# The first product by half tokens, earlier weight loads, and halo copies moved from GpSimd to VectorE

## The chip, the cores and the metric

The kernel runs on one core of a Trainium2 chip. The metric is the device time of one execution in microseconds (us). Here a profile's span is about 1.7 us shorter than the time of the same execution. Engines are named as in the profile: PE is TensorE's matmul unit, PEld its weight load, DVE is VectorE, ACT is ScalarE, POOL is GpSimd, SP is SyncE.

With each execution the mean granted TensorE clock over the span is given, 1.00 being full speed.

## The reference, cut to what matters

```python
xn = layernorm(x)                       # x: 2048 tokens x 1024, bf16
s  = attention(xn) @ wo                 # 32 heads, each token sees 8 tokens, 2 apart
g  = silu((silu(xn @ w1) * (xn @ w3)) @ w2)     # inner width 3584
return x + s * g
```

The attention of a token looks back at most 14 tokens. The kernel works on chunks of 512 tokens, so each chunk of keys and values carries a *halo*: the last few columns of the chunk before it, copied to the front of the tile.

## The kernel before

The large products are done as two-by-two block products with seven block products in place of eight, which needs sums of the inputs (`xs`, for example, are sums of blocks of the normalised x). The parts concerned:

```python
def spin(ps, n):                        # n dummy matmuls of 512 columns on zeros
    ...
def first_two(key, A, b11, b21, snap, e11, mid=lambda: None, busy=0):
    pa = []
    for g in range(2):
        pa.append(bank2(f"a{key}{g}"))
        spin(pa[g], busy if g == 0 else 0)
        for i in I:
            mm(pa[g][:, i], A[g][0][i], b11, True)
        act_copy(snap[g], pa[g][:])
    mid()
    ...
def halo(t, js):
    nc.gpsimd.tensor_copy(out=t[:, js, 0:HALO], in_=t[:, js, CH:CH + HALO])

def fetch_v(c, js):                     # called at the end of each half of values(c - 1)
    halo(vT, js)
    anchor["pool"] = nc.gpsimd.dma_start(out=vT[:, js, HALO:], in_=v_dram[c, :, js])
...
x_load(0)
wq0 = qkv_load(0, 0, slot(2, (4, D)))
x_load(1)
wq1 = qkv_load(0, 1, slot(6, (4, D)))
for st in range(NST):                   # normalise the four 128-token tiles
    (ln_act if st == 2 else ln_dve)(0, [st])
...
tps = [ln_tp(0, st, [], busy=(5, 0, 1, 1)[st]) for st in range(NST)]    # transposes on PE
for a in I:                             # copy the transposes out of PSUM
    ...
wk0 = qkv_load(1, 0, slot(8, (4, D)))
wk1 = qkv_load(1, 1, rows(0, 4).rearrange("p (k n) -> p k n", k=4))
...
TPE = ()
qkv_load(2, 0, wve[0][:])
for st in range(NST):                   # second chunk of x: normalise, transpose by DMA
    ln_dve(1, [st])
    ...
    if st == 1:
        qkv_load(2, 1, wve[1][:])
```

Near the end of the kernel, the step that PE waits for. One tile, `dsp`, gets a copy on ScalarE, an add on VectorE and a Silu on ScalarE; then the next such copy follows on ScalarE:

```python
def c22(gp):
    sp5 = k4(f"dsp{b}_{gp}")
    act_copy(sp5[:], pe[gp][:])
    with hp():
        anchor["v"] = nc.vector.tensor_add(sp5[:], pb[gp][:], sp5[:])
        silu(g_tile(b, 1, 1, gp), sp5[:])
```

## Time and profile before

| kernel before | value |
|---|---|
| median of the three runs | 726.93 us (725.63 to 726.95) |
| median of all 29 runs made beside the experiments | 726.25 us (725.3 to 727.53) |
| span of its profile | 725.4 us |
| PE busy | 715.2 us, 99% of the span |
| first useful matmul | 12.23 us |
| body (first product with `xs`) starts | 34.05 us |
| PE's part in the chain that ended last is over | 713.91 us (PE itself ends at 719.51) |

Three stretches have to be told apart: the *head*, up to 34 us, where input arrives, is normalised and transposed, and the first halves of three products run; the *body*, from the first matmul on `xs` to the end of PE's part in the chain that ended last, which lasted 679.86 us; and a tail of last sums and stores. Head, body and tail follow each other, so a gain in either of the first two is a gain in the time, unless the other takes it back.

### The profile page before, as it was taken

How to read it: one execution, taken by the hardware profiler on the slowest of the kernel's cores; microseconds unless marked ns; L12 is line 12 of the kernel's file. 1: busy time of each engine (PE TensorE's matmuls, PEld its weight loads, DVE VectorE, ACT ScalarE, POOL GpSimd, SP SyncE). 2: the span in 40 equal slices, each digit the busy share in tenths (PEclk: the TensorE clock that was granted, in tenths of full speed). 3: DMA queues.
4: the chain of work that ended last, by engine and by line, in shares of the span. 5: the costliest groups of instructions: out<-in, count | busy, mean ns of one | idle time of the engine just before them, and what ended most of it. 6: DMA issues, size and time to landing. Idle time of an engine off the chain costs nothing.

```text
span 725.4 us, 8725 instructions
## 1 busy us (share of the span) xinstructions
PE 715.2 (99%) x3335; PEld 344.1 (47%) x3335; DVE 622.8 (86%) x678; ACT 313.9 (43%) x325; POOL 111.7 (15%) x171
## 2 busy tenths in 40 slices
PE   8999999999999999999999999999999999999996
PEld 4655656554444444444444444444444444444442
DVE  8795879779879878978999999969859989978984
ACT  5654434356555556554545312034364573020233
POOL 0011100011310300332212010000434006020011
PEclk9999999999999999999999999999999999999999
DMA  9966156877755453566756556469799445564515
GB/s 325 278 155 171 59 188 215 266 237 255 225 176 180 145 174 116 178 189 199 248 166 229 184 160 219 144 203 379 175 282 321 144 136 160 167 195 140 188 27 111
DMA packets 120137, 139.77 MB, mean 193 GB/s; under 512 B 18592, under 2 KB 95392, under 8 KB 119456
## 3 DMA queue, kind: packets, MB, share of 16 engines
q1 hardware_dynamic: 105552, 97.27, 44.1%
q0 software_dynamic: 14544, 41.95, 18.8%
q8 instruction: 26, 0.43, 0.2%
q14 instruction: 15, 0.12, 0.1%
HBM read 96.21 MB, written 38.80 MB: 186 GB/s over the span
## 4 chain that ended last, share of the span: by engine, by line
PE 92%; DVE 3%; ACT 2%; DMA 1%; issue 1%; SPq 0%; DVEq 0%; ACTq 0%
PE bm L149 20%; PE am L149 13%; PE em L149 13%; PE db L149 10%; PE bq L149 9%; PE de L149 7%; PE da L149 7%; PE eq L149 5%; PE aq L149 3%; PE wb L149 2%; PE we L149 2%; PE wa L149 2%; DVE stats L250 1%; DMA wve<-in_A_wqkv_dram 1%; PE af L149 1%
## 5 line engine op out<-in xcount | busy, mean ns | idle before, releaser
L149 PEld LDWEIGHTS <-wring 128*128 128x128 f16 (+1 forms) x1824 | 187.9, 103 | 207.5 <-issue 1.9
L149 PEld LDWEIGHTS <-h_sb 128*128 128x128 f16 (+1 forms) x1056 | 109.6, 104 | 119.4 <-issue 2.0
L149 PE MATMUL bm<-xs,wring 128*128 128x512 f16 x504 | 117.4, 379 | 0.1
L149 PE MATMUL am<-xT,wring 128*128 128x512 bf16 x336 | 79.7, 379 | 0.1
L149 PE MATMUL db<-wring,h_sb 128*128 128x512 f16 x336 | 73.2, 379 | 0.0
L474 DVE TENSOR_TENSOR BC<-Ep,vT 128x2048 bf16<-128x2048 bf16 x56 | 66.7, 1219 | 0.1
L419 DVE TENSOR_TENSOR pt<-qt,kT 128x4096 bf16<-128x4096 bf16 x24 | 55.0, 2290 | 0.7
L657 DVE TENSOR_TENSOR um<-em,um 128x1024 f32<-128x1024 f32 x28 | 34.2, 1223 | 20.9 <-PE em L149 20.0
L659 ACT ACTIVATE g<-um 128x1024 bf16<-128x1024 f32 x28 | 29.6, 1057 | 48.2 <-DVE um L657 48.2
L149 PE MATMUL da<-wring,h_sb 128*128 128x512 bf16 x224 | 49.0, 379 | 0.0
L460 POOL DMA_DIRECT2D Ep<-pb x64 | 37.9, 599 | 53.7 <-DVE pb L456 46.6
L149 PE MATMUL bm<-h_sb,wring 128*128 128x512 f16 x168 | 39.7, 379 | 0.0
L149 PE MATMUL em<-xs,wring 128*128 128x512 f16 x168 | 39.7, 379 | 0.0
L149 PE MATMUL em<-xT,wring 128*128 128x512 bf16 x168 | 39.7, 379 | 0.0
L484 DVE TENSOR_TENSOR oT<-oT,BC 128x2048 bf16<-128x2048 bf16 x32 | 39.0, 1220 | 0.4
L159 ACT COPY bm<-am 128x1024 f32<-128x1024 f32 x28 | 27.9, 998 | 26.0 <-PE am L149 26.0
L159 ACT COPY pm<-em 128x1024 f32<-128x1024 f32 x28 | 28.4, 1013 | 20.1 <-PE em L149 20.1
L159 ACT COPY um<-bm 128x1024 f32<-128x1024 f32 x28 | 28.4, 1013 | 19.2 <-PE bm L149 19.2
L678 ACT CAST g<-bm 128x1024 bf16<-128x1024 f32 x28 | 28.3, 1010 | 17.4 <-PE bm L149 17.4
L672 DVE TENSOR_TENSOR h_sb<-bm,pm 128x1024 bf16<-128x1024 f32 x21 | 25.6, 1218 | 5.1 <-PE bm L149 5.0
L421 DVE TENSOR_TENSOR pt<-pt 128x2048 bf16<-128x2048 bf16 x24 | 29.3, 1222 | 0.4
L962 POOL DMA_DIRECT2D out_dram<-h_sb x12 | 15.1, 1512 | 94.7 <-DVE h_sb L961 94.6
(197 smaller groups left out, 1019.5 us busy)
## 6 DMA issues: line engine op xcount, KB each, us to landing
wring<-in_B_w_dram SPq DMA_DIRECT2D x61, 512.0 KB, 4.5
wring<-t_dram SPq DMA_DIRECT2D x16, 512.0 KB, 3.7
t_dram<-wring POOLq DMA_DIRECT2D x14, 512.0 KB, 4.6
wring<-t_dram SPq DMA_DIRECT2D x16, 384.0 KB, 5.1
wring<-in_B_w_dram SPq DMA_DIRECT2D x12, 384.0 KB, 4.0
wring<-in_A_x_dram SPq DMA_DIRECT2D x16, 256.0 KB, 4.7
Ep<-pb POOLq DMA_DIRECT2D x64, 64.0 KB, 4.6
wring<-in_A_wo_dram SPq DMA_DIRECT2D x8, 512.0 KB, 5.7
```

The source lines that it names most:

```text
L149: anchor["pe"] = nc.tensor.matmul(ps, lhsT=lhs[k], rhs=rhs[k], start=(first and k == 0), stop=(k == n - 1), skip_group_check=not first,)
L159: nc.scalar.copy(out=out_, in_=in_)
L419: nc.vector.tensor_mul(p_t[:], q[:], kT[:, :, o:o + CH])
L421: nc.vector.tensor_add(p_t[:, 0:4, :], p_t[:, 0:4, :], p_t[:, 4:8, :])
L460: nc.gpsimd.dma_start(out=pr[c][r:P:NR, :, sq * P:(sq + 1) * P], in_=pb[sq * 32:(sq + 1) * 32, :, :])
L474: nc.vector.tensor_mul(dst, E[:, w, :].unsqueeze(1).to_broadcast([P, n, CH]), vT[:, js, o:o + CH])
L484: nc.vector.tensor_add(A, A, B if w0 else C)
L657: v = nc.vector.tensor_add(su2[:], pe[:], su2[:])
L659: nc.scalar.activation(out=hl["g"][:, :, CH:], in_=su2[:], func=ACTF.Silu)
L672: anchor["v"] = nc.vector.tensor_add(h[:, :, CH:], pb[:], sp5[:])
L678: nc.scalar.copy(out=hl["g"][:, :, 0:CH], in_=pb[:])
L962: nc.gpsimd.dma_start(out=rows_, in_=g, accum_op=ALU.add)
```

## The change

The intent is to start the first product on two of the four token tiles while the other two are still being prepared, to have the weights there in time, and to take the halo copies off GpSimd.

```diff
     x_load(0)
     wq0 = qkv_load(0, 0, slot(2, (4, D)))
+    wq1 = qkv_load(0, 1, slot(6, (4, D)))
+    wk0 = qkv_load(1, 0, slot(8, (4, D)))
     x_load(1)
-    wq1 = qkv_load(0, 1, slot(6, (4, D)))
-    for st in range(NST):
-        (ln_act if st == 2 else ln_dve)(0, [st])
...
-    tps = [ln_tp(0, st, [], busy=(5, 0, 1, 1)[st]) for st in range(NST)]
...
+    ln_dve(0, [0])
+    ln_act(0, [1])
+    ln_dve(0, [2])
+    ln_dve(0, [3])
+    def p1(g, th):                      # a quarter of the first product: 256 tokens
...
+    spin_in(0, 0, 5)
+    tpose(0, 0); tpose(0, 1); untp(0, 0, dve_copy); untp(0, 1, sc_copy)
+    tpose(1, 0); tpose(1, 1); untp(1, 0, sc_copy);  untp(1, 1, sc_copy)
+    tpose(2, 0); tpose(2, 1); untp(2, 0, dve_copy)
+    p1(0, 0)
+    tpose(3, 0); tpose(3, 1); untp(3, 0, dve_copy); untp(2, 1, sc_copy); untp(3, 1, dve_copy)
+    p1(1, 0)
+    p1(0, 1)
+    p1(1, 1)
...
-    TPE = ()
-    qkv_load(2, 0, wve[0][:])
+    TPE = (3,)                          # one tile of the second chunk transposed by PE
+    for h in I:
+        qkv_load(2, h, wve[h][:])
...
     def halo(t, js):
-        nc.gpsimd.tensor_copy(out=t[:, js, 0:HALO], in_=t[:, js, CH:CH + HALO])
+        nc.vector.tensor_copy(out=t[:, js, 0:HALO], in_=t[:, js, CH:CH + HALO])
```

(The `tpose` and `untp` lines stand one to a line in the kernel.) Cut here: the root and reciprocal of the normalisation get high priority for the first two chunks, and the weight sums of `wq` are tied behind a copy of the transposes. Six dummy matmuls fall away, one each before the transposes of tiles 2 and 3 and four before the first product.

More of the change, by code (lines that the diff above doesn't have):

```diff
@@ L165, in flush, with first_two @@
             pend.pop(0)()
-    def first_two(key, A, b11, b21, snap, e11, mid=lambda: None, busy=0):
-        pa = []
+    def first_two(key, A, b11, b21, snap, e11, mid=lambda: None, pa=None):
+        have, pa = pa, pa or []
         for g in range(2):
-            pa.append(bank2(f"a{key}{g}"))
-            spin(pa[g], busy if g == 0 else 0)
-            for i in I:
-                mm(pa[g][:, i], A[g][0][i], b11, True)
-            act_copy(snap[g], pa[g][:])
+            if have is None:
+                pa.append(bank2(f"a{key}{g}"))
+                for i in I:
+                    mm(pa[g][:, i], A[g][0][i], b11, True)
+                act_copy(snap[g], pa[g][:])
         mid()
@@ L251, in ln_dve @@
             nc.vector.bn_aggr(out=mv[:, i, :], in_=stats[:])
-        nc.scalar.activation(out=rstd[:], in_=mv[:, :, 1], func=ACTF.Sqrt, bias=eps_t[:], scale=1.0)
-        nc.vector.reciprocal(out=rstd[:], in_=rstd[:])
+        with hp() if c < 2 else nullcontext():
+            nc.scalar.activation(out=rstd[:], in_=mv[:, :, 1], func=ACTF.Sqrt, bias=eps_t[:], scale=1.0)
+            nc.vector.reciprocal(out=rstd[:], in_=rstd[:])
         for i, st in enumerate(sts):
@@ L297, in xn_sums @@
         nc.vector.tensor_sub(o[:, 2], b22, b12)
-        nc.vector.tensor_sub(o[:, 3], b21, o[:, 1])
+        anchor["xs"] = nc.vector.tensor_sub(o[:, 3], b21, o[:, 1])
     def B_of(b11, b21, b22, o):
@@ L986 @@
     qt[0] = att_tile((NJ, CH), BF16, "qt0")
-    tps = [ln_tp(0, st, [], busy=(5, 0, 1, 1)[st]) for st in range(NST)]
-    for a in I:
-        for st in range(NST):
-            (nc.vector.tensor_copy if st < 2 else nc.scalar.copy)(
-                out=xT[:, a, :, st * P:(st + 1) * P], in_=tps[st][:, a].rearrange("p (k t) -> p k t", k=KH),
-            )
-    wk0 = qkv_load(1, 0, slot(8, (4, D)))
+    snap = [oT[:, i // 2, 4 * (i % 2):4 * (i % 2) + 4].rearrange("p j n -> p (j n)").bitcast(FP32).rearrange("p (i n) -> p i n", i=2) for i in range(4)]
@@ new lines, with tpose, untp @@
+    tpb = {}
+    def tpose(st, a):
+        key = a, st // 2
+        if key not in tpb:
+            tpb[key] = bank2(f"tp{a}{st // 2}")
+        tp = tpb[key]
+        for k in range(KH):
+            nc.tensor.matmul(
+                tp[:, st % 2, k * P:(k + 1) * P], lhsT=xt[0][:, st, (a * KH + k) * P:(a * KH + k + 1) * P], rhs=ident[:],
+                start=(k == 0), stop=(k == KH - 1), skip_group_check=True,
+            )
+    def untp(st, a, eng):
+        with hp():
+            r = eng(out=xT[:, a, :, st * P:(st + 1) * P], in_=tpb[a, st // 2][:, st % 2].rearrange("p (k t) -> p k t", k=KH))
+        if eng == dve_copy:
+            anchor["x"] = r
@@ new lines @@
+    dve_copy, sc_copy = nc.vector.tensor_copy, nc.scalar.copy
+    ln_dve(0, [0])
+    ln_act(0, [1])
+    ln_dve(0, [2])
+    ln_dve(0, [3])
+    pf = {}
+    def p1(g, th):
+        if g not in pf:
+            pf[g] = bank2(f"af0{g}")
+        cols = slice(th * 2 * P, (th + 1) * 2 * P)
+        w = wq0.rearrange("p k (c two j) -> p k two j c", two=2, j=4)
+        for i in I:
+            for k in range(KH):
+                nc.tensor.matmul(
+                    pf[g][:, i, cols], lhsT=w[:, k, 0, 2 * g + i, :], rhs=xT[:, 0, k, cols],
+                    start=(k == 0 and th == 0), stop=(k == KH - 1), skip_group_check=True,
+                )
+        act_copy(snap[g][:, :, cols], pf[g][:, :, cols])
@@ new lines, in spin_in @@
+    def spin_in(st, a, n):
+        tpb[a, st // 2] = bank2(f"tp{a}{st // 2}")
+        spin(tpb[a, st // 2], n)
+    spin_in(0, 0, 5)
+    tpose(0, 0)
+    tpose(0, 1)
+    untp(0, 0, dve_copy)
+    untp(0, 1, sc_copy)
+    tpose(1, 0)
+    tpose(1, 1)
+    untp(1, 0, sc_copy)
+    untp(1, 1, sc_copy)
+    tpose(2, 0)
+    tpose(2, 1)
+    untp(2, 0, dve_copy)
+    p1(0, 0)
+    tpose(3, 0)
+    tpose(3, 1)
+    untp(3, 0, dve_copy)
+    untp(2, 1, sc_copy)
+    untp(3, 1, dve_copy)
+    p1(1, 0)
@@ L1006 @@
                 )
-        if st == 1:
-            qkv_load(2, 1, wve[1][:])
     x_load(2)
@@ L1012 @@
     sq = [sq[:, q] for q in range(3)]
-    snap = [oT[:, i // 2, 4 * (i % 2):4 * (i % 2) + 4].rearrange("p j n -> p (j n)").bitcast(FP32).rearrange("p (i n) -> p i n", i=2) for i in range(4)]
     Bq = B0, B_of(xT1[0], xT1[1], xT1[3], xs1)
@@ L1022 @@
                   snap[2 * t:2 * t + 2], [qkv_copy(t, 0, 2 * g) for g in range(2)],
-                  *((lambda: None, 4) if t == 0 else (lambda: None, 0)))
-    tp1(*TPE)
-    qkv_sums(wq0, wq1, sq)
+                  *((lambda: None, [pf[0], pf[1]]), (lambda: None,), (lambda: tp1(*TPE),))[t])
+    with behind("x"):
+        qkv_sums(wq0, wq1, sq)
     xn_sums(xT[:, 0], xT[:, 1], b12, xT[:, 2], xs)
```

## The prediction

> **What bounds the kernel now.** I read the page first, then the waits of TensorE (PE), the chain in order of time, the timelines of both ends, and the row of the halo copy.
>
> ```profile
> span 725.4 us, 8725 instructions
> PE 715.2 (99%) x3335; PEld 344.1 (47%) x3335; DVE 622.8 (86%) x678; ACT 313.9 (43%) x325; POOL 111.7 (15%) x171
> PE 92%; DVE 3%; ACT 2%; DMA 1%; issue 1%; SPq 0%; DVEq 0%; ACTq 0%
> ```
>
> PE is the bound: busy for 715.2 of 725.4 us, and 92% of the chain that ended last. A change that leaves the matmuls of the body alone can win only what PE does not spend on them: the stretch before the body, and PE's waits, which the view of waits lists whole:
>
> ```profile
> PE warm L141 <- DVE warm L138: 1.3, 1, 1.3
> PE de L149 <- ACT dsp L159: 1.1, 1, 1.1
> PE af L149 <- DMA wve<-in_A_wqkv_dram: 0.4, 1, 0.4
> PE tp L281 <- DVE wring L255: 0.4, 1, 0.4
> PE tp L281 <- ACT wring L275: 0.3, 1, 0.3
> PE af L149 <- DMA wring<-in_A_wqkv_dram: 0.2, 1, 0.2
> ```
>
> The beginning, from PE's timeline (start, duration, what):
>
> ```profile
> 9.96 1.07 PE L281 MATMUL tp<-ident,wring 128*128 128x128 bf16 x16 [0.29 <-ACT wring L275]
> 11.13 1.04 PE L141 MATMUL af<-warm 128*128 128x512 bf16 x4
> 12.23 3.61 PE L149 MATMUL af<-xT,wring 128*128 128x512 bf16 x16
> 16.09 7.12 PE L149 MATMUL af<-xT,wring 128*128 128x512 bf16 x32 [0.24 <-DMA wring<-in_A_wqkv_dram]
> 30.54 3.67 PE L149 MATMUL af<-xT,wve 128*128 128x512 bf16 x16 [0.42 <-DMA wve<-in_A_wqkv_dram]
> 34.05 1.89 PE L149 MATMUL eq<-xs,h_sb 128*128 128x512 f16 x8
> ```
>
> The first useful product starts at 12.23, six groups of 16 matmuls follow with two waits for weights between, and the body starts at 34.05. From there PE is all but unbroken until 713.9. So the start of the body moves the end one for one, if nothing later has to wait.
>
> The one late wait, near the end, from the timelines of POOL, DVE and PE:
>
> ```profile
> 644.15 4.57 POOL L396 COPY vT<-vT 128x64 bf16<-128x64 bf16 x1 [30.50 <-DVE BC L474]
> 649.02 0.77 POOL L410 DMA_DIRECT2D vT<-v_dram  x1 [0.30 <-POOL vT L396]
> 654.66 1.22 DVE L474 TENSOR_TENSOR oT<-Ep,vT 128x2048 bf16<-128x2048 bf16 x1 [6.03 <-DMA vT<-v_dram]
> 673.70 1.22 DVE L825 TENSOR_TENSOR dsp<-db,dsp 128x1024 f32<-128x1024 f32 x1
> 675.92 0.99 ACT L159 COPY dsp<-de 128x1024 f32<-128x1024 f32 x1
> 676.96 6.20 PE L149 MATMUL de<-wring,h_sb 128*128 128x512 bf16 x28 [1.09 <-ACT dsp L159]
> ```
>
> Read downwards: a halo copy of 64 elements a partition takes 4.57 us on GpSimd, the reload of the values is issued only after it, VectorE idles 6.03 us for that reload, so the add into dsp is late; ScalarE, in order, does its Silu after that add and only then the second dsp copy, for which PE waits 1.09 us. The halo is thus on the path after all.
>
> [...] six copies of one size took
>
> ```profile
> L396 POOL COPY vT<-vT x6: 969/1289/4572, 297.6 to 644.2; 128x64 bf16<-128x64 bf16 x6
> ```
>
> while VectorE's products beside them kept 1215 to 1226 ns. [...] (3.61-0.38)/15 = 215 ns and, for the transposes, (1.07-0.22)/15 = 57 ns. [...] in the first 30 us these run near 390 GB/s, and the second wq half, by bytes the fourth megabyte, held PE until 16.09.
>
> **The change, part by part.** The order of instructions shows where each part fell.
>
> (a) Half tokens. Before, all four token tiles are transposed and copied, then 16 matmuls of 512 columns run from 12.23. After, the first 8 matmuls of 256 columns need tiles 0 and 1 alone. They cost 32 x 109 = 3.49 us against 16 x 216 = 3.46: nothing. Their start: tile 1 is now normalised on ScalarE, with its input some 0.7 us before tile 2's (4.2 for 4.91), yet the VectorE steps between put its last pass at 8.6 to 9.85, as now (8.66). Then ScalarE does one small root (0.3) and two copies of 0.6, of which the second completes the half: 11.3. First quarter to 12.2; transposes of tile 3 (8 x 57 = 0.46) to 12.6; three quarters to 15.25. The second half of the product starts there instead of 16.09, because wq1 now goes ahead of x's second chunk and lands some 2.7 us earlier (one megabyte at 390 GB/s). Dropping the 6 warm-up matmuls costs nothing: they filled waits. Gain 0.85.
>
> (b) Loads. The second wve half was issued at 24.01, behind transposes, and landed 30.49; now it is issued before them, and its bytes (8.4 MB from the start) are there by about 27. It takes away the hole at 30.54, 0.58 us (30.54 - 26.50 - 16 x 0.216).
>
> (c) One of four tiles of the second chunk is transposed by PE: 8 x 57 = 0.46 us on the path, against two fewer of eight DMA transposes.
>
> PE alone thus reaches the body at 15.25 + 5 x 3.456 + 0.46 = 33.0, 1.05 us earlier.
>
> (d) What takes some back. The body's first eight matmuls need xs[0], the next eight xs[1], the third VectorE sum in a row. Before, those sums began at 31.95 (after 3.97 us idle, for a transpose) and xs[1] was done at 35.45, for a matmul at 35.78: little slack. After, x's second chunk lands two megabytes later (5.4 us), so its normalisation begins at 17.4 instead of 11.6, but the three sums of wq are done before it and the idle time is used. Adding up the order after it (some 8 us of normalising, 5 sums of 1.2) the xs sums begin at 31.0 to 31.5, and need 31.1 to cost nothing. The PE transposes of tile 3 need that tile at 29.1; I get 28.6. I take off 0.4: the body gains 0.65.
>
> (e) Halo on VectorE: nine copies. A VectorE operation on 128 fp32 elements takes 0.29 us (the mask add), so at most 9 x 0.3 = 2.7 us of VectorE in 725, in background work, on no path. Late in the kernel: the halo stands two operations later in VectorE's order, so ends near 646.6 instead of 648.72; the reload lands at 646.8 + 5.6 = 652.4 instead of 654.66, and VectorE has two more products behind it by then. The add into dsp moves from 673.7 to about 669, ScalarE is free for the second dsp copy near 671.5, and PE wants it at 675.9. The wait of 1.09 goes whole, with 3 us to spare.
>
> Sum: 0.65 + 1.09 = 1.74. Time: 726.93 - 1.7 = 725.2 us.
>
> **The rivals.** First, *the body's start stays at 34 us*: the later x chunk, through normalisation, transposes and xs sums, replaces the weights as what ends the head. For it: 0.33 us of slack at 35.78 and a second chunk 5 us later. Against: 4 us of VectorE idle before those sums, two fewer DMA transposes. It would leave 1.1 alone: 725.8; two microseconds late, 727.8. Second, *the order on VectorE costs elsewhere*: the halo waits in line behind long products (2.29 us for scores), so the keys' reload starts later, and VectorE (86%, near 100% from 554 to 634) falls behind PE. For it: GpSimd's copies of keys are mostly 0.3 us, so there is little to win there. Against: elsewhere PE waits for nothing from 35 to 676. It would make 726 to 728. Third, *the late wait is hidden anyway or comes back*: if dsp is held by something else, only the head counts: 726.3. Fourth, *the head wins more*, if the half starts below 11 us and nothing holds xs: 724.5.
>
> **Range and chances.** Head 0.65, give or take 0.9; late wait 1.1 in five cases of six; the runs before spread over 1.3 us. So 723.7 to 727.0 for 8 in 10. Two per cent is 14.5 us: PE idles 10.2 us in all, so a win of that size is impossible without fewer matmuls; a loss needs a stall that nothing shows. Faster 0.01, same 0.98, slower 0.01.
>
> **What would show it.** Right: first 256-column matmul near 11.3; second half of the first product near 15.3; no wait of PE for weights; body ("eq" with xs) near 33.4; no wait of "de" for the dsp copy; halo copies on VectorE of 0.3 us or less with the late vT wait below 3 us; PE busy time about equal. Wrong: "eq" at 34 or later with a wait for VectorE's xs or the transposes; PE's tile-3 transposes waiting for VectorE; new waits of PE between 35 and 680; or a dsp wait that stays.

The quotients 215 and 57 ns are for one matmul of 512 columns and one of the transposes (128 columns), and "these" at 390 GB/s are the transfers. The 216 and 109 ns of step (a) are borne out by later traces: (7.07 - 0.38)/31 = 0.216 us in the run with the halo copies alone, and (2.79 - 0.27)/23 = 0.110 us for 256 columns in the changed kernel. The 390 GB/s holds for 10 to 20 us alone (391).

## The result, and the profile after

| | before, same rounds | changed |
|---|---|---|
| median of 6 runs | 726.22 us (725.63 to 726.95) | 725.2 us (724.57 to 726.58) |
| ratio, 95% interval | 1 | 0.9986 (0.9973 to 0.9999) |
| PE's part in the chain that ended last is over (profile) | 713.91 | 711.79 |

A ratio here is the mean time of one kernel's fast runs over that of the other's fast runs of the same rounds, so not quite the ratio of the medians. The median fell on the predicted 725.2, but the next sections show that a large part of this was an average of two modes of the clock, and that the baseline of the prediction was on the high side.

The page of the changed kernel, its span and its engines:

```profile
span 723.4 us, 8708 instructions
PE 710.8 (98%) x3299; PEld 345.6 (48%) x3353; DVE 623.7 (86%) x687; ACT 314.8 (44%) x329; POOL 96.1 (13%) x162
```

PE is the bound as before. Its busy time of 710.8 is too low, because 54 matmul records are missing (3299 against 3353 weight loads). A later profile of the same kernel with all 3353 has 713.0, so 2.2 us less than before. GpSimd has lost nine instructions and 15.6 us, while VectorE has gained nine instructions and 0.9 us.

From the view of PE's waits (total, times, longest), one that has grown and one that is new, both of the head:

```profile
PE tp L997 <- DVE wring L256: 1.5, 2, 1.3
...
PE tp L997 <- ACT xT L1004: 0.3, 1, 0.3
```

Neither `wq` nor `wve` nor the `dsp` copy is in that view any more. The grown wait, 1.3 us at the longest, is for the normalisation of a tile; it now stands after tile 0's transposes, and no dummy matmul fills it. In the first profile of before the wait for VectorE's part was 0.4 us, in the second 1.5, but there two dummies followed. (The wait at the very start, for the zeros of the dummies, is 1.3 us as before.)

The head of the changed kernel, from the timelines of PE and VectorE (start, duration, what):

```profile
11.42 1.03 PE L1022 MATMUL af<-xT,wring 128*128 128x256 bf16 x8
...
15.37 7.07 PE L149 MATMUL af<-xT,wring 128*128 128x512 bf16 x31
...
29.27 0.61 PE L282 MATMUL tp<-ident,wring 128*128 128x128 bf16 x8
31.01 1.23 DVE L296 TENSOR_TENSOR xs<-h_sb,xT 128x2048 f16<-128x2048 bf16 x1 [0.34 <-ACT h_sb L288]
33.18 1.89 PE L149 MATMUL eq<-xs,h_sb 128*128 128x512 f16 x8
```

The first useful matmul starts 0.81 us earlier than the 12.23 of before, the second half of the first product 0.72 us earlier than 16.09, and the body 0.87 us earlier than 34.05. The sum that the body's first matmul needs starts at 31.01 and does not hold PE up.

The late chain, from the timelines of VectorE, GpSimd and ScalarE:

```profile
645.49 0.17 DVE L397 COPY vT<-vT 128x64 bf16<-128x64 bf16 x1
645.96 0.77 POOL L411 DMA_DIRECT2D vT<-v_dram  x1 [30.40 <-DVE vT L397]
653.58 1.22 DVE L475 TENSOR_TENSOR oT<-Ep,vT 128x2048 bf16<-128x2048 bf16 x1 [3.26 <-DMA vT<-v_dram]
670.10 1.22 DVE L826 TENSOR_TENSOR dsp<-db,dsp 128x1024 f32<-128x1024 f32 x1
672.32 0.99 ACT L159 COPY dsp<-de 128x1024 f32<-128x1024 f32 x1
```

The halo takes 0.17 us where it took 4.57. The reload is issued 3.06 us earlier (645.96 for 649.02), the add into `dsp` starts 3.60 us earlier (670.10 for 673.70), and the second `dsp` copy is done before PE asks. The nine halos are two groups; this is the one with the long outlier before, from the view of groups:

```profile
L397 DVE COPY vT<-vT x6: 173/174/176, 316.7 to 645.5; 128x64 bf16<-128x64 bf16 x6
```

### The profile page after: what moved, and what is told of

Its sections match the earlier page's. It is cut to its first block, busy times and chain, and to the rows that moved or that the text cites. A ratio compares the mean times of both kernels' runs of the same rounds, so it can differ in the third digit from the quotient of the medians.

```text
span 723.4 us, 8708 instructions
## 1 busy us (share of the span) xinstructions
PE 710.8 (98%) x3299; PEld 345.6 (48%) x3353; DVE 623.7 (86%) x687; ACT 314.8 (44%) x329; POOL 96.1 (13%) x162
## 4 chain that ended last, share of the span: by engine, by line
PE 95%; ACT 2%; DVE 1%; issue 1%; DMA 1%; SPq 0%; DVEq 0%; ACTq 0%
PE bm L149 20%; PE am L149 13%; PE em L149 13%; PE db L149 10%; PE bq L149 9%; PE de L149 7%; PE da L149 7%; PE eq L149 5%; PE aq L149 3%; PE af L149 2%; PE wb L149 2%; PE we L149 2%; PE wa L149 2%; DMA wring<-in_A_x_dram 1%; PE af L1022 1%
## 5 line engine op out<-in xcount | busy, mean ns | idle before, releaser
L149 PEld LDWEIGHTS <-wring 128*128 128x128 f16 (+1 forms) x1808 | 185.7, 103 | 205.4 <-issue 1.6
L673 DVE TENSOR_TENSOR h_sb<-bm,pm 128x1024 bf16<-128x1024 f32 x21 | 25.6, 1218 | 5.1 <-PE bm L149 5.0
L483 DVE TENSOR_TENSOR BC<-BC 128x2048 bf16<-128x2048 bf16 x24 | 29.3, 1221 | 0.4
```

Source lines behind the costliest of these rows:

```text
L149: anchor["pe"] = nc.tensor.matmul(ps, lhsT=lhs[k], rhs=rhs[k], start=(first and k == 0), stop=(k == n - 1), skip_group_check=not first,)
L483: nc.vector.tensor_add(B, B, C)
L673: anchor["v"] = nc.vector.tensor_add(h[:, :, CH:], pb[:], sp5[:])
```

## The experiments

Twelve runs in three groups, each group on one chip with its own runs of the kernel before. All gave correct outputs. The theory was that the gain has two separate parts, an earlier body and a late wait that goes; the rivals were that one of the two is nothing, or that something else (landing of loads, the clock) makes the difference.

### The kernel before, looked at again

No edit.

> The kernel before once more, for a second profile. Theory (both savings are fixed holes in TensorE's program, not noise): the body (first eq with xs) starts within 0.2 us of 34.05 again, the second dsp copy again makes TensorE wait 1.0 to 1.2 us, the last values halo on GpSimd again takes over 4 us. Rival (the holes are luck of one execution): the dsp wait is missing or the body starts more than 0.5 us away.

Measured: 725.76 us (one run), clock 0.999. From its waits and from VectorE's timeline:

```profile
PE de L149 <- ACT dsp L159: 0.2, 1, 0.2
...
653.34 1.23 DVE L474 TENSOR_TENSOR oT<-Ep,vT 128x2048 bf16<-128x2048 bf16 x1 [5.11 <-DMA vT<-v_dram]
```

The same kernel had 1.1 us of that wait in its first profile and 0.2 here. The reload of the values let VectorE go on at 653.34 and not at 654.66, with no change of code. PE waited for no weight either; the hole at `wve` of the first profile was gone. Both waits on which the prediction rests vary from run to run.

### The changed kernel, again

No edit.

> The changed kernel against the kernel before, same chip, five rounds. Theory: ratio 0.9975 to 0.999 (1.0 to 1.9 us less), body at 33.2, no dsp wait. Rival (what is left is only the granted clock): ratio 1.000 with an interval around it.

Measured: 726.69 us median (726.44 to 726.92) with all five runs at clock 0.995, ratio 1.0008 (0.9994 to 1.0022). Five in six runs of the result were at 0.999. So on this chip the changed kernel gained nothing, and its profile shows where. The view of windows gives for each stretch its length, then the busy time of PE, PEld, DVE, ACT and POOL (instructions in brackets), then the granted clock, the DMA share and GB/s:

```profile
7.00:11.00 4.00, 1.82 (x24) 1.35 (x25) 3.96 (x13) 2.53 (x6) 0.00 (x0) 1.00 1.02 329
11.00:15.00 4.00, 3.90 (x27) 3.29 (x25) 1.44 (x3) 2.00 (x4) 0.00 (x0) 0.57 1.05 397
```

After a stretch in which PE was busy for only 1.82 of 4 us the granted clock fell; by single microseconds it was 0.50 from 12 to 15, and 1.00 again from 15 on. The second half of the keys' product began 1.54 us later than in the first profile (23.81 for 22.27), though the first quarter began 0.11 us earlier.

### Halo copies alone on VectorE

```diff
 # in the kernel before
     def halo(t, js):
-        nc.gpsimd.tensor_copy(out=t[:, js, 0:HALO], in_=t[:, js, CH:CH + HALO])
+        nc.vector.tensor_copy(out=t[:, js, 0:HALO], in_=t[:, js, CH:CH + HALO])
```

> The kernel before with the halo copies alone moved to VectorE. Theory: body start unchanged at 34.05, the dsp wait of 1.1 us gone, TensorE's last matmul about 1.1 us earlier, ratio 0.9985 (725.1). Rival 1 (the late wait is held by something else): wait stays, ratio 1.000. Rival 2 (copies on VectorE cost elsewhere): ratio above 1.000, with new TensorE waits between 35 and 660.

Measured: 725.49 us (724.97 to 726.22), ratio 0.9991 (0.9979 to 1.0004), so some 0.65 us less, not resolved. There is no wait for `dsp`, and the body lasts 678.89 us. One line of PE's timeline shows what the old head does when the weights land early:

```profile
26.01 7.07 PE L149 MATMUL af<-xT,wve 128*128 128x512 bf16 x32
```

All 32 matmuls of the values run without a break, where the first profile of before had a hole of 0.58 us. The body began at 32.92, earlier than the 33.18 of the changed kernel, with the old head.

### The new head alone

```diff
 # in the changed kernel
     def halo(t, js):
-        nc.vector.tensor_copy(out=t[:, js, 0:HALO], in_=t[:, js, CH:CH + HALO])
+        nc.gpsimd.tensor_copy(out=t[:, js, 0:HALO], in_=t[:, js, CH:CH + HALO])
```

> The changed kernel with the halo copies back on GpSimd. Theory: body at 33.2 as in the changed kernel, the dsp wait of about 1.1 us is back, the last values halo takes over 4 us [...]; ratio 0.9988 (about 0.9 us less than before). Rival (the head's gain is lost again later, waits behind the same VectorE work): ratio 1.000.

Measured: 726.27 us (725.12 to 727.37), ratio 1.0001 (0.9988 to 1.0013); the clocks were 0.999 twice (725.44 and 725.12), 0.997 twice and 0.995 once. From the waits and GpSimd's timeline of its profile, taken at 0.999:

```profile
PE de L149 <- ACT dsp L159: 0.5, 1, 0.5
...
643.03 4.57 POOL L397 COPY vT<-vT 128x64 bf16<-128x64 bf16 x1 [30.33 <-DVE BC L475]
```

With the copy back on GpSimd the long halo and the wait for `dsp` are back, and nothing else of the late chain was touched. That the halo's engine makes this wait is thereby shown. Its size here was 0.5.

### The changed kernel, a third time

No edit; on the chip of the next three runs, for comparison.

> The changed kernel once more, as the control of this group. New theory: its time has two modes, by whether TensorE's granted clock falls to 0.50 for some 3.5 us in the first 20 us (body then starts near 34.6 instead of 33.1): each run near 725.0 with mean clock 0.998 or more, or near 726.7 with mean clock 0.995 or 0.996. Rival (slow chips, or late waits): the spread shows in the body, not in the first 35 us.

Measured: 725.13 us (724.42 to 726.86), ratio 0.9992 (0.998 to 1.0004). Two of six runs were at clock 0.995 and took 726.67 and 726.86; the other four, at 0.998 to 1.0, took 724.42 to 725.33. Nothing lies between. The two modes thus occur on one chip with one program.

### Dummy matmuls put back into the changed kernel

```diff
 # in the changed kernel
     untp(0, 1, sc_copy)
+    spin_in(2, 0, 5)
     tpose(1, 0)
```

The five dummy matmuls stand between the transposes of tile 0 and the next ones, for which PE waits.

> The changed kernel with five dummy matmuls put back, in the 1.3 us hole of TensorE after tile 0's transposes. Theory (the six dummy matmuls that the change removed kept the clock up): granted clock 1.00 throughout, no run in the slow mode, all runs below 725.8, median 724.9, ratio 0.998; body at 33.2 to 33.5. Rival (the clock falls for another reason): slow-mode runs remain, as many as in the control.

Measured: 725.07 us (724.88 to 725.82), ratio 0.9988 (0.9976 to 1.0), all five clocks at 0.998 or more. The same stretch of the head in the view of windows:

```profile
7.00:11.00 4.00, 2.40 (x23) 1.44 (x24) 3.55 (x12) 2.55 (x5) 0.00 (x0) 1.00 1.02 368
```

The first useful matmul started at 11.36 and the body at 33.04, for 11.42 and 33.18 in the first profile of the changed kernel, so in the profiles the dummies cost nothing that shows.

### Dummy matmuls taken out of the kernel before

```diff
 # in the kernel before
-    tps = [ln_tp(0, st, [], busy=(5, 0, 1, 1)[st]) for st in range(NST)]
+    tps = [ln_tp(0, st, [], busy=(5, 0, 0, 0)[st]) for st in range(NST)]
...
-                  *((lambda: None, 4) if t == 0 else (lambda: None, 0)))
+                  *(lambda: None, 0))
```

> The kernel before without its six dummy matmuls between the transposes and ahead of the first product (five at the start stay). Theory: it gets the slow mode too, some or all runs with 0.50 clock for some 3.5 us and 1.5 us longer: ratio 1.001 to 1.002. Rival (only the gaps of the half-token order matter): no fall of the clock, ratio 1.000.

Measured: 727.37 us (725.94 to 729.52), ratio 1.0019 (1.0004 to 1.0033), slower with an interval that leaves out 1. Three of six clocks were 0.994 to 0.996. In its profile:

```profile
7.00:11.00 4.00, 1.24 (x16) 0.90 (x16) 3.34 (x13) 3.46 (x9) 0.00 (x0) 1.00 1.02 379
```

The clock stood at 0.50 from about 12 to 18.7. One caution: in that run a tile of x also came late, and the first useful product began at 14.14, so its 729.52 is not the clock alone. But the old head, too, falls into the lower clock when its dummies go, which the kernel before did in none of 29 runs.

### Tile 1 hurried, on top of the dummy matmuls

```diff
 # in the changed kernel with the dummy matmuls
-            nc.vector.tensor_mul(v[:, 3], v[:, 0], v[:, 2])
+            anchor["lv"] = nc.vector.tensor_mul(v[:, 3], v[:, 0], v[:, 2])
...
-    ln_dve(0, [3])
+    with behind("lv"):
+        ln_dve(0, [3])
...
-    qkv_sums(wk0, wk1, sk)
+    with behind("xs"):
+        qkv_sums(wk0, wk1, sk)
```

> The changed kernel with the five dummy matmuls, with tile 1's two small VectorE steps ahead of tile 3's statistics, and with the sums of the key weights behind the xs sums. Theory (tile 1's last pass on ScalarE waits 1.7 us for VectorE's order, 8.99 for 7.25): that pass starts near 7.8, the first 256-column matmul near 10.7, body near 32.6; 0.5 us less than with the dummy matmuls alone. Rival (weights or xs hold the body): first matmul earlier, body start as with the dummy matmuls alone, with a wait for a transfer or for VectorE.

Measured: 725.57 us (725.0 to 725.71), ratio 0.999 (0.9977 to 1.0003): a miss. VectorE's small steps for tile 1 did come earlier, but PE's waits have a new line:

```profile
PE tp L997 <- DVE xT L1004: 1.2, 1, 1.2
```

Tiles 0 and 1 share one PSUM tile for their transposes, and the transposes of tile 1 now waited for VectorE's copy of tile 0 out of it. The first useful matmul started at 11.56, no earlier than without the edit.

### The whole-token start in the changed kernel

```diff
 # in the changed kernel: the half-token block goes, the block of before comes back
-    ln_dve(0, [0])
-    ln_act(0, [1])
...
-    p1(1, 1)
+    for st in range(NST):
+        (ln_act if st == 2 else ln_dve)(0, [st])
+    tps = [ln_tp(0, st, [], busy=(5, 0, 1, 1)[st]) for st in range(NST)]
...
+        spin(first[g], 0 if g else 4)
+        for i in I:
+            mm(first[g][:, i], qkv_A(wq0, wq1, [wq0] * 3, g)[0][i], B0[0], True)
```

The key sums were tied behind `xs` as well, because the half-token block's copies could no longer hold them.

> The changed kernel's loads, tile-3 transposes and VectorE halo, but the first product over full tokens with its six dummy matmuls, as in the kernel before (the key sums stand behind the xs sums, so that tile 3 is not late). Theory (the half-token start gains little: the transposes it moves between the quarters and its own start take 0.5 of the 1.0 us): first product at 12.2, no wait for weights, body at 33.4 to 33.6, 0.3 us later than the changed kernel in its fast mode, no fall of the clock; median near 725.4, ratio 0.999. Rival (half tokens gain the whole 1 us): body at 34.0 or later, 726.2.

Measured: 727.43 us (726.8 to 728.03), ratio 1.0012 (0.9999 to 1.0024). It is confounded: without the copies that order VectorE's work, statistics of the third chunk of x came ahead of the `xs` sums in VectorE's order, and VectorE stood 8.04 us waiting for that chunk. PE then waited 1.21 us for `xs`, and the body began at 35.37. Without that wait PE would have asked at 34.0 by my working, which is 25.6 us after its transposes of tile 0 started (8.38); the half-token head takes 25.61 us for the same. As a test of the time this run says little. As a test of when tile 0 is ready it says more, as shown below.

### The old order of loads in the changed kernel

```diff
 # in the changed kernel
     wq0 = qkv_load(0, 0, slot(2, (4, D)))
-    wq1 = qkv_load(0, 1, slot(6, (4, D)))
-    wk0 = qkv_load(1, 0, slot(8, (4, D)))
     x_load(1)
+    wq1 = qkv_load(0, 1, slot(6, (4, D)))
...
     p1(1, 1)
+    wk0 = qkv_load(1, 0, slot(8, (4, D)))
...
-    for h in I:
-        qkv_load(2, h, wve[h][:])
+    qkv_load(2, 0, wve[0][:])
...
+        if st == 1:
+            qkv_load(2, 1, wve[1][:])
```

> The changed kernel with the loads in the order of the kernel before. Theory (the loads' order is what takes away the waits for weights): first 256-column matmuls near 11.2 as in the changed kernel, then TensorE waits for the second wq half until about 16 (0.3 to 0.8 us) and perhaps for the second wve half; body between 33.3 and 34.1; also no better than the changed kernel in its fast mode. Rival (the weights land in time anyway, as they did in two of four profiles with the old order): no wait for weights, body at 33.0.

Measured: 726.37 us (725.79 to 727.21), ratio 0.9997 (0.9985 to 1.001). In its profile PE waited for no weight, and the body lasted the same 678.61 us. But three of its five runs were at clock 0.995, the profiled one among them (0.50 from 11 to 14.3): a slower PE asks for its weights later (the second half of the first product began at 16.41, for 15.37 in the first profile of the changed kernel), so the missing wait is weak evidence, and the clock explains part of the time. At full clock two runs remain, 726.37 and 725.79, too few to say whether the load order is worth anything on average.

### No transpose of the second chunk on PE

```diff
 # in the changed kernel
-    TPE = (3,)
+    TPE = ()
```

> The changed kernel with all four tiles of the second chunk transposed by DMA. Theory (six DMA transposes end being issued at 29.3, 1.3 us each, and two more would land near 34): TensorE is 0.46 us shorter, but the xs sums wait for the last transposes, xs[0] is done near 33.5 or later and the body starts at 33.6 to 34.6 with a wait for VectorE's xs; slower than the changed kernel's fast mode by 0.5 to 1.5. Rival (transposes land in time): body at 32.7, 0.4 faster.

Measured: 727.11 us (725.37 to 727.99), ratio 1.0006 (0.9992 to 1.002). PE's waits have two new lines:

```profile
PE bq L149 <- DVE xs L297: 0.6, 1, 0.6
PE eq L149 <- DVE xs L296: 0.5, 1, 0.5
```

The 0.45 us of transposes saved come back as 0.5 + 0.6 of waits for the `xs` sums, of which the first began at 31.51 instead of 31.01 (in a run that had started 0.57 us earlier): it waited for a DMA transpose. So in this profile this part of the change pays for itself, with x's second chunk loaded after two weights. Four of its runs stood at 0.997 and three of them took 727.11 to 727.99; why is open.

### The dummy matmuls once more, on another chip

The edit of the first run with dummy matmuls put back, for the count of clocks.

> The changed kernel with five dummy matmuls put back, again, on whatever chip this is. Theory: again no run in the slow mode, all five below 726.0 with mean clock 0.997 or more, median 725.0 give or take 0.3, ratio 0.998 to 0.999. Rival: a run near 726.7 at clock 0.995.

Measured: 725.35 us (724.95 to 727.46), ratio 0.9987 (0.9974 to 1.0). One of five runs fell to 0.995 and was the slowest, 727.46.

## Why the prediction was right or wrong

The total was right and inside its range. Of its steps, three held in mechanism and size, two were mis-sized, and one was wrong. They follow in its own order.

**(a) Half tokens: the times held, the reason was partly another.** First 256-column matmul 11.3 predicted, 11.42 measured; second half of the first product 15.25 predicted, 15.37 measured. But this step took the readiness of the tiles as unchanged, and it did change. From VectorE's timeline, before, the first statistics and the normalisation of tile 0:

```profile
3.52 1.88 DVE L250 BATCH_NORM_STATS2 stats<-wring 128x6 f32<-128x512 bf16 x3 [2.28 <-DMA wring<-in_A_x_dram]
...
7.30 0.53 DVE L255 TENSOR_SCALAR wring<-wring,mv,rstd 128x1024 bf16<-128x1024 bf16 x1
```

And the same in the changed kernel:

```profile
3.32 1.29 DVE L250 BATCH_NORM_STATS2 stats<-wring 128x6 f32<-128x512 bf16 x2 [2.09 <-DMA wring<-in_A_x_dram]
...
6.98 0.53 DVE L256 TENSOR_SCALAR wring<-wring,mv,rstd 128x1024 bf16<-128x1024 bf16 x1
```

Before, three statistics run ahead of tile 0's first result; after, only its own two. VectorE's timeline shows one instruction after another, so each statistic of another tile that stands ahead of tile 0's normalisation adds its own 0.64 us, and its wait for x too. From the start of the statistics to PE's transposes of tile 0 the five profiles with the old block took 4.37, 4.81, 4.45, 6.00 (no dummies) and 4.97 us (whole token), and the nine with the new block 3.25 to 4.32, on average 3.8 for 4.9. So tile 0 is ready about 1.1 us earlier. It is the block and not the loads: the whole-token run had the new loads and 4.97, the run with old loads had the new block and 3.52.

After that the half-token start gives less. From the transposes of tile 0 to the first useful matmul it takes 3.85 us where the old head took 4.34, but from there to the body 21.76 where the old head needs 20.72 if no weight is late: twice 0.45 us of transposes now lie between the products, and some 0.14 us of small gaps. The whole is 25.61 against 25.06.

**"Dropping the 6 warm-up matmuls costs nothing: they filled waits" is the step that failed.** They filled waits, and thereby kept PE busy. From the views of windows, and the count of fallen runs:

| kernel | PE busy in 7 to 11 us, of 4, in its profiles | runs with fallen clock |
|---|---|---|
| before | 3.24 and 2.19 | 0 of 29 |
| changed, dummies put back | 2.40 and 2.60 | 1 of 10 |
| changed | 2.04, 2.17 and 1.82 | 8 of 17 |
| before, without dummies | 1.24 | 3 of 6 |

Of the other new heads, those without the dummies fell in at least 4 of 15 runs, and the one with them and tile 1 hurried in none of 5.

In the 17 runs of the changed kernel the eight at 0.995 took 726.44 to 726.92, on average 726.70, and the nine at 0.998 or more 724.42 to 725.34, on average 724.95. The fall costs 1.75 us, more than the whole head was to gain. By the granted clock of single microseconds the fall lasted 3.40 us in the second profile of the changed kernel, 3.42 in the run with old loads, and 6.82 in the old head without dummies. The matmuls bear it out: eight transposes took 1.06 us from 12.75 in the second profile of the changed kernel, 0.61 from 12.29 in the first.

The stretch from 7 to 11 us does not tell the runs apart: the second profile of before had 2.19 and kept its clock, as did the new head alone with 1.94; the run with old loads had 2.17 and lost it. In the second profile of the changed kernel, the 3.41 us just before the fall and the 3.41 us after:

```profile
8.16:11.57 3.41, 1.66 (x19) 1.30 (x20) 3.02 (x9) 2.69 (x5) 0.00 (x0) 1.00 1.01 357
11.57:14.98 3.41, 3.41 (x23) 2.87 (x21) 1.20 (x2) 1.43 (x3) 0.00 (x0) 0.50 1.05 396
```

PE's longest single wait there was 1.28 us. But the first profile, which did not fall, has a stretch just as idle:

```profile
8.10:11.51 3.41, 1.58 (x19) 1.12 (x18) 3.20 (x11) 2.52 (x5) 0.00 (x0) 1.00 1.00 377
```

So how busy PE was in such a stretch does not decide alone, and why one run fell and another with the same program did not is not shown. What the runs show is the counts of the table: without the dummies the clock fell more often.

**(b) Loads: over-read from one profile.** The hole at `wve` is gone, as predicted. But of the kernel before and its halo version, three profiles at full clock, one alone had it. What was called a fixed 0.58 us is a matter of when the load lands. With the loads in the old order and the new head no weight was late either, though PE was slowed there. The prediction's rate was over-read too: in its profile the transfers ran at 391 GB/s from 10 to 20 us, but at 270 before and 238 from 20 to 30.

**(c) One tile on PE: held.** 0.46 predicted, 0.45 measured (29.27 to 29.72), and the run without it shows what it buys.

**(d) What takes some back: held.** The `xs` sums were predicted at 31.0 to 31.5 and tile 3 at 28.6; they came at 31.01 and 28.39. The body was predicted near 33.4 and began at 33.18. (The prediction lets PE run until 713.9; it runs until 719.51, and 713.91 is where it leaves the last chain, which changes none of the sums.) At full clock five profiles of the new head (with or without dummies and the new halo) have 32.50 to 33.19, mean 32.97, and three of the old have 32.92 to 34.05, mean 33.54. The head's gain at full clock is thus about 0.6 us, as predicted (0.65), by eight profiles whose ranges overlap, though as 1.1 for tile 0 less 0.55 for the rest, plus what late weights cost the old head in some runs.

**(e) Halo on VectorE: mechanism right, size off.** Predicted at most 0.3 us for each copy, 0.17 to 0.19 measured; the add into `dsp` predicted at 669, measured 670.10; the wait predicted to go whole, and it did. It was to leave the wait of VectorE for the values under 3 us, and left 3.26: the reload was issued where it should be, but landed in 7.6 us, not 5.6. The mis-sized term is the 1.09. Over four profiles with GpSimd's halo the wait for `dsp` was 1.1, 0.2, 0.5 and 0.6, on average 0.6, and the timed halo run gave 0.65 (not resolved). The prediction took the largest for the rule.

How a copy of 64 elements a partition comes to take 4.57 us on GpSimd can be seen in part at another long one in the kernel before, from the timelines of GpSimd and VectorE:

```profile
248.09 4.77 POOL L396 COPY kT<-kT 128x128 bf16<-128x128 bf16 x1 [7.52 <-DVE pt L419]
...
252.29 0.42 DVE L425 TENSOR_TENSOR Es<-pt 128x512 bf16<-128x512 bf16 x1
253.09 1.23 DVE L657 TENSOR_TENSOR um<-em,um 128x1024 f32<-128x1024 f32 x1 [0.38 <-PE em L149]
```

VectorE ran one product behind the other until 252.71, then waited 0.38 us for PE; the copy ended at 252.86, in that gap. The halo at 644.15 ended at 648.72, 0.09 us after VectorE's product of 647.41 to 648.63. VectorE's products of 2048 elements beside these two copies kept their 1.22 us. The other five copies of values, 0.97 to 1.29 us, likewise ended about 0.1 us after a VectorE product. So these seven copies end with a VectorE product; what ties the two together is not shown. A gap is not needed: three of the five ended with VectorE's next product already begun (which then took 1.25 to 1.26 us, above the 1215 to 1226 ns of the prediction), and why two copies were passed over by several products and the rest were not stays open.

**The sum.** 1.74 us was predicted, from a start of 726.93. Over all 29 runs the kernel before has a mean of 726.29, so 0.64 of the distance to 725.2 was the luck of three runs. Over 17 runs the changed kernel has 725.77: a gain of 0.5 us (an estimate, as the runs are not all of the same rounds). It is made of 1.34 at full clock (726.29 less 724.95), and of 8/17 x 1.75 = 0.82 that the fallen clock takes back. The 1.34 fits about 0.6 of head and 0.6 of halo.

**The rivals.** None came as told. The body's start was not held by x's second chunk; VectorE's order cost nothing in the body, which lasts 678.61 us in the changed kernel in every profile at either clock, against 678.94 and 679.86 in two profiles of the kernel before; and the late wait did not come back. What happened, a lower clock, was not among the rivals, though PE's busy time in the head, counted with and without the dummies, could have suggested it.

**A version that may be better than both.** The changed kernel with five dummy matmuls ahead of tile 1's transposes took 725.07 and 725.35 us in two groups, with ratios of 0.9988 and 0.9987 to before, and a mean of 725.43 over ten runs: 0.9 us below before and 0.3 below the changed kernel. Both intervals end at 1.0, so the step is small and just at the edge of what was resolved. At full clock its nine runs average 725.21, 0.26 above the nine of the changed kernel, so what it gains is the rarer fall of the clock: with tile 1 hurried, the runs with dummies fell in 1 of 15. The chips differ, though: five of the eight falls of the changed kernel came from the one chip where the dummies were not tried.

**What stays open.** Whether five falls in five runs on one chip, against one of six and two of six elsewhere, is more than luck; whether the load order is worth anything on average; and why the run without PE's tile 3 was slow at clocks of 0.997. The mean clock cannot tell there: it also counts the time after PE's end at 719.51 (there the clock stood at 0.50 from 723 us on), which alone brings the first profile of before to 0.998, while one fall of 3.40 us takes 0.0023 (0.5 x 3.40 of 724.8), so a run at 0.997 may hold a fall or not.

## What to carry to other kernels

Matmuls that compute nothing may still be doing work: after six of them were dropped here, 8 of 17 runs had a mean clock of 0.995 and took 1.75 us longer than the rest. So look at the granted clock of many runs, not of one profile, before and after dropping them. Waits of some tenths of a microsecond that end on a transfer belong to a run and not to a kernel (the hole at `wve` was there in one of three profiles, and the wait for `dsp` was 0.2 to 1.1 us in four), so two or three profiles of the kernel before should be read before such a wait is counted as a gain. A tiny copy on GpSimd beside a series of VectorE products took up to 4.57 us here and held up a whole chain; look for groups whose longest duration is many times their shortest.
